# A filler stream with one gate/up tile fewer: its work moves to the seven-product stage, its order and its rate change

## The chip, the cores and the metric

The kernel runs on one core of one Trainium2 chip. The metric is the time of one execution in device microseconds (us). Three runs of the kernel before gave a median of 1049.95 us, between 1048.82 and 1053.6 us. A core has five engines that run side by side and wait for each other through semaphores: PE (TensorE, the matrix unit), DVE (VectorE), ACT (ScalarE), POOL (GpSimd) and SP (SyncE, which here only issues DMAs). In the profile, PEld is the loading of weights into PE.

## The reference: what is computed

One transformer block whose two branches are added: sliding-window attention and a gated feed-forward part, both on the same normalized input.

```python
def _A_ref(x, wqkv, wo):                       # S = 2048 tokens, D = 640, H = 32 heads of Dh = 20
    q, k, v = split(x @ wqkv)
    scores = einsum("bhqd,bhkd->bhqk", q, k) * Dh ** -0.5
    mask = (i - j >= 0) & (i - j < 256)        # causal window of 256
    p = softmax(where(mask, scores, -1e9))
    return reshape(einsum("bhqk,bhkd->bhqd", p, v)) @ wo
def _B_ref(x, w_gate, w_up, w_down):           # Df = 1728
    return (gelu(x @ w_gate) * (x @ w_up)) @ w_down
xn = layernorm(x)
return x + _A_ref(xn, ...) + _B_ref(xn, ...)
```

## The kernel before

**Numbers.** Weights and activations are split into a high and a low part, and each dense product is three matmul passes: high times high, low times high, high times low. A dense product of one 128-column weight tile with one chunk of C = 512 tokens has a depth of 640 = 5 x 128, so it is 15 matmuls of 512 columns (`dense_steps`, L102, its matmul in L106). There are NC = 4 chunks.

**Tiles of weights.** The q and k projections are 10 tiles, worked off in pairs ("qk", i): q tile i and k tile i + 5. The gate and up weights are NF = 14 tiles of 128 columns each (the last, 13, holds the 64 left over of both). One full gate/up tile over all four chunks costs 2 x 4 x 15 = 120 dense matmuls in the plain way.

**Stages in order of time.** First the layer norm, the transposes and the first projections (about 0 to 96 us). Then the attention (about 96 to 550 us). Then what is left of the feed-forward products ("gate/up stage", 550 to 809 us). Last, the down and the output projections (`ps` in L1216, from 809 us on).

**The attention stage** (`attention`, L802) is written out by hand for PE, ACT, DVE and POOL. It has NU = 32 units, one for each of 8 groups of four heads and 4 chunks of tokens; a unit has NS = 14 slots. In a unit PE does four kinds of small matmuls: `ps_m` (L491, raw scores from which DVE takes a maximum, L501), `ps_n` (L518, moves the maxima into place; ACT then sends them to the q rows by a DMA, L521), `ps_e` (L556, shifted scores, of which ACT makes P with an exponential, L558) and `ps_o` (L599, P times V, `av_unit`, called in slot 0 of the next unit). Twelve `ps_e` pieces of a unit come two at a time in the odd slots. POOL blanks the masked corners of P (`clear`, L571 and L574) in the slot after, and adds the two halves of the result (`join`, L609).

**The filler.** Between these small matmuls PE is given dense products from a generator, `filler` (L689): each slot pulls RATE / NS of them (`pull_fill`, L797), 31.2 for a unit; a matmul of 320 columns counts 0.65. `filler` yields in this order: two projections that are left over, then `sets`: the q/k pairs 1, 2, 3, the gate/up tile 0, the q/k pair 4, the gate/up tiles 1 and 2. The products for V of the second half of the heads (`ps_v`) come in when slot V1_SLOT = 169 is past. The weights of the next set are split by ACT and POOL in the meantime (`split_later`, L630; L635, L640), alternately into two pools (`pools`, L686). A q/k product is followed by two ACT steps, one of DVE and one of POOL (`save_qk`, L247; POOL's is L258) and a store to DRAM by SP (L267); a gate/up product by steps of ACT and DVE (`gate_up_fill`, L645). On top POOL forms sums of activations for the next stage, three steps in a unit (`x_sums`, L726; L737, stored in L741).

**Queues.** SP issues its DMAs in program order: the results of the previous unit (L613, L614), the stores of q/k products (L267), the sums (L741), and, in slots 9 and 12, the k and the q rows of unit u + 3 (`load_stack`, L457; L466), which the maxima of that unit read first in slot 5 of unit u + 1. POOL works its list in order too.

**The gate/up stage.** The tile that is split last in the filler (13) is done in the plain way (`gate_up`, L864). Tiles NFA = 3 to 12 are done by `gate_up_pair` (L931; matmuls in L949): for two chunks together, seven products of sums of blocks take the place of eight. It has 6 + 9 + 6 + 9 + 6 + 9 + 9 = 54 dense matmuls for a pair of chunks, and 108 for a tile.

```python
    sets = [("qk", 1), ("qk", 2), ("qk", 3), ("gu", 0), ("qk", 4)]
    sets += [("gu", f) for f in range(1, NFA)] + [("gu", NF - 1)]
    ...
                if i == 0 and u:
                    av_unit(u - 1)
```

Of the kernel before, what the change touches and what calls it, by code (L numbers as in the profile page):

```python
# [28 lines left out]
SR = 3 * DH  # L29
QROWS = 64 + SR  # L30
NS = 14
RATE = 31.2
V1_SLOT = 169
MXD = 7
KSLOT = 9
LAG = 3, 5, 4, 4, 4, 4, 3, 3, 4, 3, 2, 1, 1, 1
NFA = 3
HD = D // 2
HR = 5
NQD = 9  # L40
# [26 lines left out]
def block_kernel(ctx, tc, x, wqk, wv, wgu, wdo, wdl, out):  # L67
# [131 lines left out]
    def at(slot, fn, *a):  # L199
        acts.setdefault(slot, []).append((fn, a))  # L200
# [9 lines left out]
    def flush():  # L210
        while lates:
            fn, a = lates.pop(0)
            fn(*a)
# [118 lines left out]
    def run(*gens):  # L332
        for gen in gens:
            for _ in gen:
                pass
# [121 lines left out]
    def load_stack(u, which=(0, 1)):  # L457
        g, c = divmod(u, NC)
        for m in range(80 * g // 128, (80 * g + 79) // 128 + 1):
            assert all((m + 5 * i, c) in done for i in which), (u, m)  # L460

        for i in which:
            dst, src, top, again = ((qs[u % NQ], qd[c], 1, 2), (ks[u % NK], kd[c], 0, 0))[i]
            for j in (0, 2):
                for p, part, n in ((j * 32, top, 2), (j * 32 + 2 * DH, again, 1), (64 - j * 32, 0, 3)):
                    nc.sync.dma_start(dst[p:p + DH * n, j:j + 2].rearrange("p j t -> p (j t)"),  # L466
                                      src[g, part:part + n].rearrange("s (d j) t -> (s d) (j t)",
                                                                      j=4)[:, j * C:(j + 2) * C])
# [150 lines left out]
    def load_gu(f):  # L619
        raws = []  # L620
        for i in range(2 if f < NF - 1 else 1):
            raw = wrp.tile([128, KT, 128], F32, name="wr", tag="wr")
            nc.sync.dma_start(raw, wgu[2 * f + i])
            raws.append(raw)
        return raws
# [55 lines left out]
                                   lambda k: xh[:, k, cs], lambda k: xl[:, k, cs], KT)  # L681
            defer(1, *((late, c4) if i else (c1,)))

    sets = [("qk", 1), ("qk", 2), ("qk", 3), ("gu", 0), ("qk", 4)]
    sets += [("gu", f) for f in range(1, NFA)] + [("gu", NF - 1)]
    pools = (wp, None), (hp, 2)  # L686
    rest = []
# [91 lines left out]
    NU = NG * NC  # L779
# [4 lines left out]
    def pull_max(n, slot):  # L784
        for _ in range(n):
            x = next(stream, None)
            if x is None:
                return
            max_pair(*x)
            if x[1] == 7:  # L790
                at(slot + (MXD if slot >= 0 else 4), max_end, x[0])

    def tick():
        todo = [y for t in sorted(t for t in acts if t <= now[0]) for y in acts.pop(t)]
        return sorted(todo, key=lambda y: y[0] is max_end)

    def pull_fill(n):  # L797
        debt[0] += n
        while debt[0] > 0:
            debt[0] -= next(fill, 1.0)  # L800

    def attention():  # L802
        now[0] = -1
        load_stack(0)
        load_stack(1)
        load_stack(2)
        for i, (p, k, half) in enumerate((p, k, half) for p in range(NC // 2) for k in range(2) for half in range(2)):
            for j, fn in enumerate(x_sums(p, k, half)):
                m = 10 * i + j
                at(NS * (XS0 + m // XSN) + m % XSN, fn)  # L810
        for i in range(12):
            now[0] = i - 13
            for fn, a in tick():
                fn(*a)
            if i % 2 == 0:
                pull_max(2, now[0])
            flush()
            pull_fill(2 * RAMP)
        pull_fill(GAP)
        for u in range(NU + 1):  # L820
            for i in range(NS):
                T = now[0] = NS * u + i
                for fn, a in tick():
                    fn(*a)
                if i in (0, 5, 9) or T == 3:
                    pull_max(2, T)
                if i == 0 and u:
                    av_unit(u - 1)
                    flush()
                    pull_max(2, T)  # L830
                if i % 2 and i < 12 and u < NU:
                    exp_piece(u, i - 1)
                    if i == 1 and u:
                        pull_fill(1)
                        debt[0] -= 1
                    exp_piece(u, i)
                flush()
                if u + 3 < NU and i in (KSLOT, 12):
                    load_stack(u + 3, (int(i == KSLOT),))
                pull_fill(RATE / NS)  # L840
        while acts:
            now[0] += 1
            for fn, a in tick():
                fn(*a)
            flush()
        now[0] = None
        run(fill)
        assert not acts
# [446 lines left out]
    order.__enter__()  # L1295
    raws_w = load_gu(NFA)
    banks = [psg.tile([128, C], F32, name="ps_g", tag=f"g{i}") for i in range(4)]
# [32 lines left out]

    raws_next = {NFA + 1: load_gu(NFA + 1)}
    for j, f in enumerate(range(NFA, NF - 1)):
        end = f + 1 == NF - 1
# [166 lines left out]
```

## Time and profile before

The profiled execution took 1055.0 us, and its span from the first to the last instruction was 1053.2 us.

| what | value |
|---|---|
| median of three runs | 1049.95 us (1048.82 to 1053.6) |
| profiled execution, its span | 1055.0 us, 1053.2 us |
| granted PE clock, mean of the span | 0.997 |
| busy share of the span | PE 98%, PEld 79%, DVE 70%, ACT 50%, POOL 37% |
| 98 to 550.4 us (attention): PE, ACT, DVE, POOL busy | 447.42, 302.37, 297.18, 328.52 of 452.40 us |
| 565 to 809 us (gate/up): PE, DVE busy | 244.00, 169.03 of 244.00 us |

A busy PE is not a PE at its peak: the profile models the end of a matmul, and matmuls overlap. What one matmul costs is the distance from its start to the next start. In rows of the timeline the columns are start, duration, engine, line, operation, output and inputs, shape and count; in brackets stands how long the engine was idle before, and what ended it. In rows of the chain of waits the columns are start, length, engine, output, line and count.

### The profile page before, as it was taken

What the parts mean: (1) busy time and instruction counts of PE and PEld (TensorE: products, weight loads), DVE (VectorE), ACT (ScalarE), POOL (GpSimd) and SP (SyncE); (2) the same over time, 40 slices, a digit from 0 to 9 for tenths busy, and PEclk for the clock granted to TensorE, in tenths of its full rate; (3) what the DMA queues carried; (4) which work ended last, traced back from release to release, by engine and by line L of the source; (5) the groups of instructions that cost most, each with busy time, mean ns of one, the idle gap of its engine ahead of it and who ended that gap; (6) DMA issues with size and microseconds to landing.
All of it is one profiled execution on the core that took longest, in us unless ns stands there. A gap on an engine that the chain in (4) does not pass through costs nothing.

```text
span 1053.2 us, 25694 instructions
## 1 busy us (share of the span) xinstructions
PE 1037.1 (98%) x9393; PEld 837.1 (79%) x9393; DVE 742.0 (70%) x2018; ACT 528.6 (50%) x1120; POOL 385.6 (37%) x622
## 2 busy tenths in 40 slices
PE   8999999999999999999999999999999999999998
PEld 8878666666787666666668888888888999999998
DVE  7845666667655676677736787776556869888887
ACT  4434766676666667666675232223324544343332
POOL 6021687979665767877460111101110000000000
PEclk9999999999999999999999999999999999999999
DMA  5543355555533344544125576762217874443333
GB/s 198 188 125 99 103 160 161 162 181 153 162 89 106 104 145 125 172 138 155 59 66 192 177 248 207 251 252 110 75 62 254 258 236 131 131 133 115 119 126 105
DMA packets 105192, 158.76 MB, mean 151 GB/s; under 512 B 15420, under 2 KB 60092, under 8 KB 105064
## 3 DMA queue, kind: packets, MB, share of 16 engines
q1 hardware_dynamic: 102680, 150.95, 44.3%
q10 hardware_dynamic: 2384, 6.16, 1.8%
q8 instruction: 74, 1.21, 0.5%
q14 instruction: 54, 0.44, 0.1%
HBM read 101.78 MB, written 54.92 MB: 149 GB/s over the span
## 4 chain that ended last, share of the span: by engine, by line
PE 84%; DVE 7%; DMA 3%; ACT 3%; issue 2%; POOL 1%; SPq 0%; ACTq 0%; DVEq 0%; POOLq 0%
PE ps_g L949 22%; PE ps_d L106 20%; PE ps L1216 16%; PE ps_e L556 8%; PE ps_v L106 6%; PE ps_o L599 5%; PE ps_m L491 4%; DVE junk L501 2%; PE ps_g L106 1%; DVE at L1054 1%; DVE ss L1054 1%; DMA stg<-wtd 1%; DVE wb L1054 1%; PE ps_t L184 1%; DMA qs<-qd 1%
## 5 line engine op out<-in xcount | busy, mean ns | idle before, releaser
L501 DVE CUSTOM_DVE_ANT_0 junk<-ps_m,mask 128x320 bf16<-128x320 f32 (+2 forms) x512 | 242.7, 474 | 132.5 <-PE ps_m L491 75.0
L558 ACT ACTIVATE P<-ps_e 128x512 f32<-128x512 f32 (+2 forms) x384 | 198.8, 571 | 62.1 <-PE ps_e L556 60.1
L1216 PE MATMUL ps<-wb,at 128*128 128x320 f32 x999 | 156.6, 309 | 1.5 <-DVE at L1054 1.4
L1216 PEld LDWEIGHTS ps<-wb,at 128*128 128x128 f32 x999 | 148.9, 188 | 2.4 <-DVE at L1054 1.9
L571 POOL TENSOR_SCALAR_AFFINE_SELECT P<-P 128x256 f32<-128x256 f32 (+1 forms) x192 | 95.4, 501 | 68.5 <-ACT P L558 65.6
L556 PE MATMUL ps_e<-qs,ks 124*128 124x128 bf16 (+2 forms) x704 | 119.0, 278 | 0.5
L106 PE MATMUL ps_d<-xh,wql 128*128 128x512 f32 x310 | 99.3, 424 | 0.0
L106 PE MATMUL ps_d<-xh,wqh 128*128 128x512 f32 x310 | 98.3, 422 | 0.0
L106 PE MATMUL ps_d<-xl,wqh 128*128 128x512 f32 x310 | 98.2, 420 | 0.0
L99 POOL TENSOR_TENSOR wql<-wr,wqh 128x640 fp32r<-128x640 f32 x12 | 19.2, 1607 | 196.1 <-PE ps_g L949 151.0
L1216 PE MATMUL ps<-wt,at 128*128 128x320 f32 x552 | 89.2, 310 | 0.8 <-DVE xr L1239 0.8
L556 PEld LDWEIGHTS <-ks 124*128 124x128 bf16 x704 | 49.6, 98 | 50.3 <-issue 35.3
L574 POOL TENSOR_SCALAR_AFFINE_SELECT P<-P 128x512 f32<-128x512 f32 (+1 forms) x144 | 78.6, 554 | 17.6 <-ACT P L558 15.8
L1216 PEld LDWEIGHTS ps<-wt,at 128*128 128x128 f32 x552 | 82.9, 188 | 1.3 <-DVE xr L1239 1.0
L1170 ACT ACTIVATE at<-ss 128x512 fp32r<-128x512 f32 x59 | 37.3, 632 | 88.1 <-DVE ss L1054 88.1
L599 PE MATMUL ps_o<-P,v 64*32 64x320 f32 (+4 forms) x2816 | 74.8, 347 | 1.7 <-POOL P L574 1.7
L258 POOL TENSOR_TENSOR pt<-r,pt 128x512 bf16<-128x512 f32 x40 | 46.8, 1169 | 70.1 <-ACT pt L254 61.7
L599 PEld LDWEIGHTS ps_o<-P,v 64*32 64x32 f32 x2816 | 50.7, 106 | 23.9 <-POOL P L574 1.6
L491 PE MATMUL ps_m<-ks,qs 60*64 60x320 bf16 (+3 forms) x1472 | 63.2, 260 | 3.8 <-DVE xl L193 1.1
L106 PEld LDWEIGHTS ps_d<-xh,wql 128*128 128x128 f32 x310 | 56.7, 191 | 10.2 <-issue 1.1
L106 PEld LDWEIGHTS ps_d<-xl,wqh 128*128 128x128 f32 x310 | 56.3, 190 | 9.9 <-issue 1.3
L106 PEld LDWEIGHTS ps_d<-xh,wqh 128*128 128x128 f32 x310 | 56.1, 190 | 9.9 <-issue 1.6
(195 smaller groups left out, 1940.8 us busy)
## 6 DMA issues: line engine op xcount, KB each, us to landing
hr<-hd SPq DMA_DIRECT2D x104, 128.0 KB
hd<-he SPq DMA_DIRECT2D x50, 256.0 KB
wr<-wgu SPq DMA_DIRECT2D x27, 320.0 KB
qs<-qd SPq DMA_DIRECT2D x64, 120.0 KB
ks<-kd SPq DMA_DIRECT2D x64, 120.0 KB
xi<-x SPq DMA_DIRECT2D x16, 320.0 KB
qs<-qd SPq DMA_DIRECT2D x64, 80.0 KB
ks<-kd SPq DMA_DIRECT2D x64, 80.0 KB
```

The lines of the kernel that those rows point to most:

```text
L106: nc.tensor.matmul(ps, a(k), b(k), start=n == 0, stop=n == 3 * nk - 1)
L258: nc.gpsimd.tensor_tensor(out=pt[:, l, :], in0=r, in1=pt[:, 1, :], op=OP.subtract)
L491: nc.tensor.matmul(ps[64 * h:64 * h + 64, col:col + w], q[rows, j, q0:q0 + 64], ks_, start=True, stop=True, tile_position=(64 * r, 64 * h))
L501: nc.vector.tensor_tensor_reduce(out=junk[:, 0:n], in0=ps[:, 320 - n:320], in1=mask[:, 320 - n:320], scale=1.0, scalar=NEG, op0=OP.add, op ...
L556: nc.tensor.matmul(ps[:, col:col + n], k[0:QROWS, j, kc:kc + 128], q[0:QROWS, j, q0:q0 + n], start=True, stop=True)
L558: nc.scalar.activation(pt[:, j, lo:hi], ps[:, lo:hi], AF.Exp, scale=SCALE)
L571: nc.gpsimd.affine_select(out=a, in_=a, pattern=[[0, n], [1, 128]], compare_op=OP.is_ge, fill=0.0, base=0, channel_multiplier=-1)
L574: nc.gpsimd.affine_select(out=a, in_=a, pattern=[[0, n], [-1, 128]], compare_op=OP.is_ge, fill=0.0, base=-1, channel_multiplier=1)
L599: nc.tensor.matmul(os[r][32 * j:32 * j + 32, qa:qb], v[rows, w0_:w0_ + 32], pt[rows, j, col + qa - q0:col + qb - q0], start=r not in begun ...
L949: nc.tensor.matmul(ps, i, j, start=first and n == 0, stop=n == len(work) - 1, skip_group_check=True)
L1170: nc.scalar.activation(hi[:, 3:7], s, AF.Copy)
L1216: nc.tensor.matmul(ps[bank][:, 0:HD], *work[bank][j], start=bank not in begun, stop=final[p, bank] == n and j == len(work[bank]) - 1, skip ...
```

## The change

Four edits. NFA is 2 in place of 3: gate/up tile 2 is no longer yielded by the filler, and the loop over `gate_up_pair` starts with it. RATE is 27.2 in place of 31.2. In `sets`, the q/k pair 4 comes ahead of the gate/up tile 0, so that all q/k pairs come first; there is one set fewer, so the pools of weights alternate the other way round from there on. In slot 0 after the last unit, `pull_fill(LAST)` with LAST = 8 is called ahead of the last `av_unit`.

```diff
-RATE = 31.2
+RATE = 27.2
+LAST = 8
 V1_SLOT = 169
 ...
-NFA = 3
+NFA = 2
 ...
-    sets = [("qk", 1), ("qk", 2), ("qk", 3), ("gu", 0), ("qk", 4)]
+    sets = [("qk", 1), ("qk", 2), ("qk", 3), ("qk", 4), ("gu", 0)]
     sets += [("gu", f) for f in range(1, NFA)] + [("gu", NF - 1)]
 ...
                 if i in (0, 5, 9) or T == 3:
                     pull_max(2, T)
                 if i == 0 and u:
+                    if u == NU:
+                        pull_fill(LAST)
                     av_unit(u - 1)
                     flush()
                     pull_max(2, T)
```

## The prediction

> **What bounds the kernel now.** I read the page first, then the busy time by stage, then the waits of PE, then the chain of waits through one attention unit. The first two rows are of the page, the next two of the busy time by stage (a stretch, its length, then busy time and count of each engine, the granted clock, the DMA share), the last three of the waits of PE between 98 and 550 us (total us, times, longest).
>
> ```profile
> span 1053.2 us, 25694 instructions
> PE 1037.1 (98%) x9393; PEld 837.1 (79%) x9393; DVE 742.0 (70%) x2018; ACT 528.6 (50%) x1120; POOL 385.6 (37%) x622
> 98.00:550.40 452.40, 447.42 (x6012) 305.79 (x6010) 297.18 (x1099) 302.37 (x663) 328.52 (x557) 1.00 0.44 132
> 565.00:809.00 244.00, 244.00 (x1077) 201.83 (x1076) 169.03 (x281) 76.04 (x143) 26.89 (x18) 1.00 0.50 175
> PE ps_o L599 <- POOL P L574: 1.7, 2, 1.1
> PE ps_m L491 <- DMA qs<-qd: 0.9, 2, 0.4
> PE ps_m L491 <- DVE mx L501: 0.7, 2, 0.4
> ```
>
> PE is busy nearly throughout in both stages that the change touches, at full clock, and waits for others for only 3.3 us in the attention. Since ends of matmuls are modelled, I check this in the chain of waits, over one unit from `ps_o` to `ps_o`:
>
> ```profile
> 421.49 2.38 PE ps_o L599 x93
> ...
> 431.88 0.54 PE ps_e L556 x4
> 432.42 1.15 PE ps_d L106 x5
> 433.57 0.45 PE ps_e L556 x4
> 434.02 1.39 PE ps_d L106 x6
> ...
> 435.81 0.39 PE ps_o L599
> ```
>
> Every piece is PE's own and each follows where the last ends: the unit (14.32 us) is a sum of PE work. One dense matmul costs 0.23 us in runs of five and six (1.15 / 5 and 1.39 / 6 = 0.232). So four fewer dense matmuls shorten a unit as long as no other engine's answer comes too late. In the gate/up stage one costs 244.00 / 1077 = 0.2266 us, without any gap.
>
> **The change part by part.**
>
> *Tile 2 out of the filler, the lower rate.* 120 dense matmuls leave the attention. The order of the built programs confirms it: 27 or 28 dense matmuls in a unit where 31 or 32 stood, while the other matmuls stand as they did. Gain if PE stays the bound: 120 x 0.232 = 27.8 us, 0.93 us for a unit of four.
>
> *Tile 2 into the gate/up stage.* 108 matmuls at 0.2266 us: 24.5 us more. DVE gets the additions of one more tile: it is busy for 169.03 of 244.00 us there, and does not set the pace. POOL's splitting of one tile moves along, into a stage where it works for 26.89 us. I cost these at nothing: PE's 24 us for a tile cover them, at 169.03 / 10 = 17 us of DVE for a tile; without that cover they would cost DVE's 17 us. The two loads of raw weights only move along SP's queue.
>
> A page gives another price. The Trainium skill (TensorE: Matmul & The Clock Gate, Back-to-back issue gap) states about 216 ns for an isolated warm matmul of 512 columns, wherever it stands; by that the swap would save 12 x 0.216 = 2.6 us and not 27.8 - 24.5 = 3.3 us, an estimate from the page. The trace has 0.2266 and 0.232 us, and decides.
>
> *Dense work ahead of the last P times V.* The timeline of PE, POOL and ACT at the end of the attention, and a row of SP's waits for the next edit:
>
> ```profile
> 544.89 0.70 PE L556 MATMUL ps_e<-qs,ks 124*128 124x128 bf16 x4
> 546.24 2.02 PE L599 MATMUL ps_o<-P,v 64*32 64x320 f32 x52 [0.65 <-POOL P L574]
> 549.34 1.12 PE L599 MATMUL ps_o<-P,v 64*32 64x320 f32 x44 [1.08 <-POOL P L574]
> 550.39 0.96 PE L106 MATMUL ps_g<-xh,wqh 128*128 128x512 f32 x3
> 542.78 1.57 POOL L99 TENSOR_TENSOR wql<-wr,wqh 128x640 fp32r<-128x640 f32 x1 [0.32 <-ACT wqh L98]
> 547.03 1.17 POOL L881 TENSOR_TENSOR wql<-wr,wqh 128x384 fp32r<-128x384 f32 x1
> 549.24 0.59 POOL L571 TENSOR_SCALAR_AFFINE_SELECT P<-P 128x256 f32<-128x256 f32 x1
> 540.01 0.60 ACT L653 ACTIVATE gs<-ps_d 128x512 f32<-128x512 f32 x1
> SPq L466 <- DMA kd<-pt: 5.8, 4, 2.4
> ```
>
> The last `ps_e` begins at 544.89 and `ps_o` at 546.24: 1.35 us, where a block of four takes 0.45, so 0.9 us are lost. `ps_o` then takes until 550.39, 4.15 us, where an undisturbed one takes 2.38: 1.8 us, because POOL splits a weight (L881) ahead of the last blanking. Together 2.7 us. In the changed order seven dense matmuls are left for this place (1.6 us, and not eight), and L881's work comes behind the last blanking. Both causes go, but two ACT steps of the filler's last product (0.6 us each) now stand between exponentials of that unit, which have no spare dense work around them: I give back 0.5 us and take 2.2 us; bounds 0 and 2.7.
>
> *q/k pair 4 first.* By itself no work: it keeps the q and k rows of the seventh head group ahead of their loads at the lower rate. What it removes is small: SP waited 5.8 us in four places for stores of k rows, off PE's path. I cost it at nothing; if the rows were late, PE would wait in `ps_m`, as below.
>
> *What is late next: the loads of q rows.* The attention's slack against SP and POOL shrinks. The busy time in one loaded unit, POOL and SP's queue in it, and PE where it reads the rows; then a place where PE did wait for such a load:
>
> ```profile
> 179.75:193.97 14.22, 14.22 (x204) 9.48 (x207) 9.63 (x37) 10.47 (x21) 13.78 (x24) 1.00 0.59 166
> 186.51 1.29 POOL L609 TENSOR_TENSOR ob<-ob,P 128x512 f32<-128x512 f32 x1
> 189.53 1.16 POOL L258 TENSOR_TENSOR pt<-r,pt 128x512 bf16<-128x512 f32 x1
> 187.83 1.42 SPq L613 DMA_DIRECT2D od<-ob  x4
> 190.72 1.26 SPq L267 DMA_DIRECT2D qd<-pt  x2
> 192.08 2.70 SPq L466 DMA_DIRECT2D ks<-kd  x6
> 194.88 2.16 SPq L466 DMA_DIRECT2D qs<-qd  x6
> 200.40 0.47 PE L491 MATMUL ps_m<-ks,qs 60*64 60x256 bf16 x16
> 164.39 3.09 SPq L466 DMA_DIRECT2D qs<-qd  x6
> 171.65 0.47 PE L491 MATMUL ps_m<-ks,qs 60*64 60x256 bf16 x15 [0.43 <-DMA qs<-qd]
> ```
>
> POOL is busy for 13.78 of 14.22 us. Its late addition (L609) holds SP's stores, its late L258 holds the next ones, and behind them in SP's queue stand the loads of k and q: the q load is issued at 194.88 to 197.04, for a use at 200.40. In the last rows the data came 171.65 - 167.48 = 4.2 us after the last issue, and PE waited. At 200.40 it did not, so the slack there lies between nothing and some 1.4 us. With the change, PE comes to this place earlier by the four matmuls of a unit and about one of the next, 1.2 us. POOL's list gets shorter only by the part that hangs on the filler: at 31.2 matmuls a unit, 2.08 q/k products of 1.16 us and the splitting of weights (240 matmuls take five pieces of 0.47 us four times: 1.2 us a unit), 3.6 us, of which 4 in 31 go: 0.47 us. So up to 1.2 - 0.47 = 0.77 us is lost in such a unit, at least nothing. The group of splitting pieces (470 ns each), and how many units are like this:
>
> ```profile
> POOL 6021687979665767877460111101110000000000
> L640 POOL TENSOR_TENSOR wql<-wr,wqh 128x128 fp32r<-128x128 f32 x65 | 29.5, 470 | 3.3 <-ACT wqh L635 3.3
> 478.31:492.64 14.33, 14.33 (x210) 9.57 (x214) 10.02 (x38) 9.50 (x19) 11.15 (x22) 1.00 0.48 146
> ```
>
> In slices six to ten (26.3 us each, 132 to 263 us) POOL stands at 7 to 9: nine units. The four units of pair 4 come earlier now; I add three, twelve in all (a later unit without q/k products has POOL at 11.15 of 14.33, with room). Bounds 0 and 12 x 0.77 = 9.2 us; I take a third, 3.0 us, since some slack is there and not every unit has two products or a weight to split.
>
> *The exponentials.* `ps_e` has two PSUM banks, so a pair waits until ACT has read the pair before:
>
> ```profile
> 432.30 1.09 ACT L558 ACTIVATE P<-ps_e 128x512 f32<-128x512 f32 x2 [0.27 <-POOL pt L258]
> 433.84 1.09 ACT L558 ACTIVATE P<-ps_e 128x512 f32<-128x512 f32 x2 [0.46 <-PE ps_e L556]
> ```
>
> ACT needs 1.09 us for a pair, starts some 0.3 us after PE (433.84 against 433.57), and with four dense matmuls between the pairs PE returns after 0.45 + 4 x 0.232 = 1.38 us: just in time. The changed order has four dense matmuls at most of these places and three in four units at the last pair, where 0.2 us each is lost: 0.8 us. Bounds 0 and 31 x 0.1 = 3 us, if the places that are just in time give way too. DVE's maxima I cost at nothing: 9.63 us of 14.22 leave room; if not, it is within that 3 us.
>
> *Sum.* -27.8 + 24.5 - 2.2 + 3.0 + 0.8 = -1.7 us. Against the profiled execution (1055.0 us, span 1053.2 us, 1.8 us around it) that is 1053.3 us; it lies 5 us above the median of the runs (1049.95 us), and from the median it gives 1048.2 us.
>
> **The rivals.**
>
> *Clean: no new waits.* -27.8 + 24.5 - 2.2 = -5.5 us, 1044.4 us. For it speaks that PE waits for only 3.3 us today, and that the attention's other engines are at 65 to 73% (297.18 to 328.52 of 452.40 us). Against it, POOL's 13.78 us in loaded units is more than the 13.3 us that a unit would last. The waits that exist, if they vanish too, would bring 1 us more.
>
> *Slower: SP's queue behind POOL sets the unit.* Place: the wait of `ps_m` for the q rows in slot 5. Price: the whole 0.93 us of a unit comes back. If it holds in some 20 of the units with sums and q/k products, 18.6 us come back: -5.5 + 18.6 = +13 us, 1063 us. It decides from twelve units on (11.2 - 5.5 = +5.7 us). For it: the lost microsecond at 171 us already has this form. Against: after it the units run without such a wait, though POOL is as full.
>
> *The attention isn't bound by PE.* Then the removal brings nothing and the added tile costs all: 24.5 - 2.2 = +22 us, 1072 us. For it: PEld is at 305.79 of 452.40 us, 68%, below POOL's 73%. Against: the chain above has only PE in it. The Trainium skill (Perfetto Trace Analysis, Identifying the Most-Contended Engine) bears on this: matmul busy time is no good measure of PE, weight-load busy time is the better one. By that rule POOL would be the engine to relieve; the starts in the chain, without a gap, speak against it here.
>
> *The last edit does nothing.* If the stall at the end only moves, 2.2 us of gain go: 1050.4 us, inside the forecast's span.
>
> **How the numbers follow.** Forecast (part of the gain eaten, between -5 and +5 us) 0.52; clean 0.24; SP behind POOL 0.19; not PE-bound 0.05. A change under 0.5% (5.2 us) is about what a measurement of this kernel can't tell from none. Clean lies just past that bound; I count most of it, 0.22, as faster, the rest and the forecast, 0.54, as the same, the other two as slower, 0.24. The range goes from 1043.4 us (clean, with today's waits gone) to 1058 us, which takes in the upper bounds of loads and exponentials (-5.5 + 9.2 + 3 = +6.7 us) and the beginning of the second rival; past it lie about 0.15.
>
> **What would show it.** Right: units of 13.4 to 13.7 us from `ps_o` to `ps_o`, with the longer ones between 130 and 260 us and a wait of `ps_m` for the q load there; 108 more `ps_g` matmuls at 0.227 us; a last `ps_o` of about 2.4 us. Wrong: units of 14 us with PE waiting for `qs<-qd` or for POOL all along (second rival), units of 13.3 us throughout (clean), or PE idle ahead of the last `ps_o` as before.

## The result, and the profile after

The changed kernel takes 1059.48 us (median of six runs, 1056.78 to 1061.18); the kernel before took 1049.96 us beside it (six runs). The ratio is 1.0078, 95% interval 1.0060 to 1.0096: slower by 0.8%, and outside the range that I gave (1043.4 to 1058.0 us). Later batches, on other occasions, put the kernel before at 1052.95, 1051.92 and 1051.63 us (19, 19 and 27 runs); against those medians the same 1059.48 us would be a loss of 6.5 to 7.9 us, but the changed kernel was not run again beside them. Its six runs fall into two groups, 1056.8 to 1057.9 and 1061.0 to 1061.2 us, and the median lies between them.

The head of the page after, and the busy time by stage (a stretch, its length, busy time and count of PE, PEld, DVE, ACT and POOL, the granted clock, DMA share and rate):

```profile
span 1058.9 us, 25671 instructions
PE 1038.9 (98%) x9381; PEld 836.4 (79%) x9381; DVE 750.7 (71%) x2029; ACT 527.4 (50%) x1120; POOL 380.0 (36%) x614
```

```profile
98.00:531.60 433.60, 424.30 (x5878) 284.58 (x5876) 289.96 (x1079) 293.86 (x647) 319.18 (x547) 1.00 0.44 131
565.00:809.00 244.00, 244.00 (x1079) 202.09 (x1078) 164.57 (x284) 71.44 (x142) 26.44 (x18) 1.00 0.47 162
```

The gate/up stage looks as before: PE without any gap, 244.00 / 1079 = 0.2261 us for a matmul, DVE at 164.57 of 244 us. The attention does not: PE is idle for 433.60 - 424.30 = 9.3 us of it, where it had been idle for 452.40 - 447.42 = 5.0 us. The waits of PE between 96 and 560 us, after:

```profile
PE ps_m L492 <- DVE mx L502: 2.5, 9, 0.4
PE ps_n L519 <- DVE mx L502: 2.3, 3, 1.7
PE ps_m L492 <- DMA qs<-qd: 1.6, 3, 0.6
PE ps_e L557 <- ACT P L559: 0.3, 2, 0.2
PE ps_m L492 <- DVE nm L511: 0.3, 1, 0.3
```

DVE is now the engine that PE waits for most: 2.5 + 2.3 + 0.3 us, where it was 0.7 us. The q rows stand at 1.6 us where they stood at 0.9. The end of the attention in the timeline after (start, duration, engine, line, operation, tensors, shape, count; in brackets idle time and what ended it):

```profile
526.86 0.87 PE L557 MATMUL ps_e<-qs,ks 124*128 124x128 bf16 x4 [0.15 <-ACT P L559]
528.02 1.29 PE L107 MATMUL ps_d<-xl,wqh 128*128 128x512 f32 x5
529.03 0.40 POOL L575 TENSOR_SCALAR_AFFINE_SELECT P<-P 128x256 f32<-128x256 f32 x1
529.24 2.45 PE L600 MATMUL ps_o<-P,v 64*32 64x320 f32 x96
529.96 1.00 POOL L884 TENSOR_TENSOR wql<-wr,wqh 128x384 fp32r<-128x384 f32 x1 [0.17 <-ACT wqh L883]
531.62 0.74 PE L107 MATMUL ps_g<-xh,wqh 128*128 128x512 f32 x2
```

All 96 matmuls of the last `ps_o` follow each other, from 529.24 to 531.62: 2.38 us, where it had been 4.15 us; dense work stands ahead of it, and the splitting of a weight (L884) comes behind the last blanking.

Spans of single executions differ by some microseconds for reasons outside the change: stretches at half clock in the first 70 us, and weights that arrive a little late at about 50 and 65 us of the last stage. So I compare stages, by the starts of PE's matmuls in the timeline, in one profiled execution of each kernel; e1_nolast, which is almost the same program as the changed kernel, repeats its stages up to the down product to 0.3 us. All times in us:

| kernel | first to last `ps_o` | last `ps_o` to gate/up | gate/up | down and output |
|---|---|---|---|---|
| before | 439.0 | 4.2 | 258.7 | 244.1 |
| after | 423.8 | 2.4 | 283.1 | 244.2 |
| e1_nolast | 424.1 | 2.7 | 282.9 | 242.3 |
| e2_lean_after | 421.3 | 2.4 | 283.1 | 244.4 |
| e3_lean_before | 438.0 | 4.1 | 258.7 | 242.4 |
| e4_two_rates | 418.7 | 3.0 | 283.0 | 244.7 |
| e5_nfa_alone | 430.2 | 3.6 | 283.0 | 244.3 |
| e8_hold | 420.6 | 2.4 | 283.1 | 241.7 |
| e9_shift | 431.2 | 2.4 | 283.0 | 243.4 |
| e10_all_but_nfa | 438.9 | 2.4 | 258.6 | 242.4 |
| e11_lean_hold | 420.3 | 2.4 | 283.1 | 243.6 |
| e12_nfa4 | 467.3 | 3.1 | 234.2 | 243.2 |
| e13_two_hold | 419.0 | 3.1 | 283.1 | 242.5 |

The added tile costs +24.4 us (forecast 24.5). Between the first and the last `ps_o` PE has 116 dense matmuls fewer (688 `ps_d` and 804, 240 `ps_v` in both); four more were saved ahead of it. At 0.232 us that is 26.9 us, and 15.2 us came. So 11.7 us of new waits stand in the attention, and the question is which.

To find them I took each piece of PE's work in the 31 units, each from one `ps_o` to the next (a block of `ps_m`, of `ps_e`, of dense work), from its start to the start of the next, and set it against the shortest usual time of pieces of the same kind and size in all the kernels (the lower eighth); what is over is put to the piece that was late. Pieces that are late by less than 0.04 us are left out, so the sum comes to 10.6 us of the 11.7. Sums in us:

| late piece | before | after | e2 lean | e4 two rates | e8 hold | e11 lean, hold | e12 four tiles |
|---|---|---|---|---|---|---|---|
| first maxima of a unit (`ps_m` around `ps_o`; DVE) | 4.7 | 6.9 | 7.0 | 5.0 | 4.6 | 4.6 | 8.1 |
| the maxima's move (`ps_n`; DVE's negation) | 0.1 | 3.0 | 0.5 | 0.4 | 1.2 | 0.5 | 0.0 |
| later maxima (`ps_m`; q rows, DVE) | 1.9 | 4.6 | 4.1 | 3.3 | 5.3 | 6.0 | 1.1 |
| shifted scores (`ps_e`; exponentials) | 6.8 | 9.6 | 10.1 | 12.0 | 9.7 | 9.5 | 5.9 |
| all | 13.6 | 24.2 | 21.7 | 20.6 | 21.0 | 20.8 | 15.5 |

Of the 10.6 us, 8.6 fall in the first twelve of the units (5.7 there before, 14.3 after), which hold most of the q/k products. From `ps_o` to `ps_o`, these twelve last 14.18 us on average in place of 14.34, the other nineteen 13.35 in place of 14.04. Three places of the changed kernel show what the lines mean.

*DVE's list, at the start of the fifth unit.* Rows of the timeline:

```profile
159.80 0.59 ACT L559 ACTIVATE P<-ps_e 128x512 f32<-128x512 f32 x1
160.27 0.60 ACT L277 ACTIVATE pt<-ps_d 128x512 bf16<-128x512 f32 x1
160.98 0.69 DVE L273 TENSOR_TENSOR r<-ps_d,pt 128x512 f32<-128x512 f32 x1 [1.09 <-ACT pt L277]
163.42 0.29 PE L492 MATMUL ps_m<-ks,qs 60*64 60x320 bf16 x1 [0.26 <-DVE mx L502]
164.06 0.33 PE L492 MATMUL ps_m<-ks,qs 60*64 60x320 bf16 x3 [0.35 <-DVE mx L502]
```

A step of DVE on a filler product (L273) stands in its list ahead of the maxima. It needs ACT's L277, which stands in ACT's list behind the exponentials. DVE stands still for 1.09 us; then this step takes 0.69 us while scores whose product began at 160.57 stand ready behind it, and PE pays when it comes back for the second block of `ps_m`. DVE has time enough; its list does not let it use that time.

*A negation, in the eleventh unit.*

```profile
250.81 0.87 POOL L641 TENSOR_TENSOR wql<-wr,wqh 128x128 fp32r<-128x128 f32 x2
251.42 3.70 DVE L511 TENSOR_SCALAR nm<-mx 128x16 bf16<-128x16 f32 x1
251.63 1.28 POOL L610 TENSOR_TENSOR ob<-ob,P 128x512 f32<-128x512 f32 x1
252.87 0.46 POOL L641 TENSOR_TENSOR wql<-wr,wqh 128x128 fp32r<-128x128 f32 x1
253.28 0.64 POOL L572 TENSOR_SCALAR_AFFINE_SELECT P<-P 128x512 f32<-128x512 f32 x1
253.87 1.22 POOL L575 TENSOR_SCALAR_AFFINE_SELECT P<-P 128x512 f32<-128x512 f32 x2
255.79 0.22 PE L519 MATMUL ps_n<-identb,nm 128*128 128x128 bf16 x1 [1.65 <-DVE mx L502]
```

The DVE instruction of 128 x 16 numbers lasts 3.70 us, and ends (255.12) when POOL's unbroken row of work ends (255.09). Its usual time is in the view of the tile `nm` (count, then shortest, middle and longest in ns), first before, then after:

```profile
L510 DVE TENSOR_SCALAR nm<-mx x32: 174/175/1203, 80.7 to 526.1; 128x16 bf16<-128x16 f32 x32
```

```profile
L511 DVE TENSOR_SCALAR nm<-mx x32: 174/176/3704, 79.2 to 508.4; 128x16 bf16<-128x16 f32 x32
```

What releases it can be counted. The traces of the fourteen kernels hold 864 such small steps of DVE (`nm<-mx` and, right behind it, `nm<-mx,nm`). 242 of them last 0.256 us or more: a POOL instruction was running at the start of every one of these, and every one ends 0.025 to 0.037 us after the end of a POOL instruction, in 236 cases of one that ran at its start. The other 622 last 0.174 to 0.185 us: at their start POOL was idle, or had at most 0.15 us left of its instruction. So a negation that starts under a POOL instruction lasts until that instruction ends. Six, this one among them, were held over one or more further POOL instructions that followed without a pause; why these and not others stays open.

*The q rows, in the fourth unit.* The chain of waits (start, length, what):

```profile
150.62 3.50 DMA qs<-qd
154.11 0.14 issue
154.25 0.47 PE ps_m L492 x11
```

The chain goes through a load of q rows, issued at 150.56 us and needed 3 us later. The timeline shows why SP came to it so late:

```profile
141.08 0.63 ACT L255 ACTIVATE pt<-r 128x512 bf16<-128x512 f32 x1
141.85 1.29 POOL L641 TENSOR_TENSOR wql<-wr,wqh 128x128 fp32r<-128x128 f32 x3
143.09 1.16 POOL L259 TENSOR_TENSOR pt<-r,pt 128x512 bf16<-128x512 f32 x1
144.28 1.76 SPq L268 DMA_DIRECT2D kd<-pt  x3
```

ACT's part of a k product is done at 141.71, but three splits of a weight stand ahead of it in POOL's list; SP waits 2.6 us for POOL's part, then stores the product, and issues the loads of k and q behind it almost without a pause until 152.27. This is the wait that the prediction had named, by the path that it had named.

### The profile page after: what moved, and what is told of

Read it like the earlier page. It is cut to its first block, busy times and chain, and to the rows that moved or that the text cites. A ratio compares the mean times of both kernels' runs of the same rounds, so it can differ in the third digit from the quotient of the medians.

```text
span 1058.9 us, 25671 instructions
## 1 busy us (share of the span) xinstructions
PE 1038.9 (98%) x9381; PEld 836.4 (79%) x9381; DVE 750.7 (71%) x2029; ACT 527.4 (50%) x1120; POOL 380.0 (36%) x614
## 4 chain that ended last, share of the span: by engine, by line
PE 83%; DVE 8%; ACT 4%; DMA 3%; issue 2%; POOL 0%; ACTq 0%; DVEq 0%; SPq 0%
PE ps_g L952 25%; PE ps L1219 17%; PE ps_d L107 15%; PE ps_e L557 7%; PE ps_v L107 6%; PE ps_o L600 5%; PE ps_m L492 4%; DVE junk L502 2%; ACT P L559 2%; PE ps_g L107 1%; DMA qs<-qd 1%; DVE ss L1057 1%; DMA hr<-hd 1%; ACT pt L277 1%; DMA out<-xr 1%
## 5 line engine op out<-in xcount | busy, mean ns | idle before, releaser
L572 POOL TENSOR_SCALAR_AFFINE_SELECT P<-P 128x256 f32<-128x256 f32 (+1 forms) x192 | 92.5, 486 | 61.1 <-ACT P L559 59.6
L100 POOL TENSOR_TENSOR wql<-wr,wqh 128x640 fp32r<-128x640 f32 x13 | 20.8, 1601 | 217.3 <-PE ps_g L952 172.4
L107 PE MATMUL ps_d<-xh,wql 128*128 128x512 f32 x270 | 87.8, 425 | 0.0
L107 PE MATMUL ps_d<-xh,wqh 128*128 128x512 f32 x270 | 87.5, 424 | 0.0
L107 PE MATMUL ps_d<-xl,wqh 128*128 128x512 f32 x270 | 85.9, 420 | 0.0
L492 PE MATMUL ps_m<-ks,qs 60*64 60x320 bf16 (+3 forms) x1472 | 66.5, 260 | 6.5 <-DVE mx L502 2.5
L981 ACT ACTIVATE hr<-hr 128x512 f32<-128x512 f32 x22 | 13.9, 632 | 111.2 <-DVE hr L955 111.2
L600 PEld LDWEIGHTS ps_o<-P,v 64*32 64x32 f32 x2816 | 50.8, 106 | 21.7 <-issue 0.9
L492 PEld LDWEIGHTS <-qs 60*64 60x64 bf16 x1472 | 29.8, 105 | 48.0 <-issue 39.6
L952 PE MATMUL ps_g<-xh,wql 128*128 128x512 f32 x198 | 66.3, 389 | 0.0
```

The source lines that it names most:

```text
L107: nc.tensor.matmul(ps, a(k), b(k), start=n == 0, stop=n == 3 * nk - 1)
L492: nc.tensor.matmul(ps[64 * h:64 * h + 64, col:col + w], q[rows, j, q0:q0 + 64], ks_, start=True, stop=True, tile_position=(64 * r, 64 * h))
L572: nc.gpsimd.affine_select(out=a, in_=a, pattern=[[0, n], [1, 128]], compare_op=OP.is_ge, fill=0.0, base=0, channel_multiplier=-1)
L600: nc.tensor.matmul(os[r][32 * j:32 * j + 32, qa:qb], v[rows, w0_:w0_ + 32], pt[rows, j, col + qa - q0:col + qb - q0], start=r not in begun ...
L952: nc.tensor.matmul(ps, i, j, start=first and n == 0, stop=n == len(work) - 1, skip_group_check=True)
```

## The experiments

**Less work for POOL, and so for SP behind it.** Six of the ten POOL steps of `x_sums` are left out, so that the sums lack the low parts, in the changed kernel and in the kernel before.

```diff
 def s2():
-    pool(live[1], live[1], el[:, k, b], OP.add)
+    pass
 # likewise in s3, s5, s7, s9, s10: the terms of the low parts
```

> The changed kernel with six of the ten POOL steps of each sum of activations left out (the sums, and so the output, are incomplete; their stores to DRAM stay). POOL has about 1.3 us less to do in a unit that forms sums. Theory 1 (in the first eleven units POOL's list, and SP's queue behind it, is too long for a unit of 13.4 us): most of the loss there goes, the units 1 to 11 come down from 14.1 to about 13.5 us on average, and the kernel takes 1051 to 1054 us. Theory 2 (the dense products end at other slots than those the delays were set for, and so DVE's and ACT's in-order lists meet the maxima and exponentials at a worse place, whatever POOL does): 1057 to 1060 us, units 1 to 11 at about 14.

> The kernel before with the same six of ten POOL steps left out (its output is incomplete too): the control. Theory 1: little to win, since the units of 14.3 us hold POOL's list: 1046 to 1050 us, so that the two lean kernels stand 2 to 6 us apart, where the full ones stand 9.5 us apart. Theory 2: the same 1046 to 1050 us, but still 9 us less than the lean changed kernel.

Measured: 1057.8 us, ratio 1.0061 (1.0043 to 1.0080), in the changed kernel; 1052.45 us, ratio 0.9998 (0.9980 to 1.0015), in the kernel before. The attention got 2.5 us shorter in the one and 1.0 us in the other. The table says where: the held negation is gone (3.0 to 0.5 us), everything else stays. At the same place of the program:

```profile
251.30 1.30 POOL L610 TENSOR_TENSOR ob<-ob,P 128x512 f32<-128x512 f32 x1
252.46 0.58 DVE L511 TENSOR_SCALAR nm<-mx 128x16 bf16<-128x16 f32 x1
252.55 0.46 POOL L641 TENSOR_TENSOR wql<-wr,wqh 128x128 fp32r<-128x128 f32 x1
253.60 0.64 POOL L572 TENSOR_SCALAR_AFFINE_SELECT P<-P 128x512 f32<-128x512 f32 x1 [0.58 <-ACT P L559]
```

POOL has a pause from 253.01 to 253.60, and the negation ends at 253.04. In both kernels its end lies 0.03 us behind POOL's. The wait for q rows stays, at 1.2 us in place of 1.6. The three splits of a weight (1.29 us) stand ahead of POOL's step in this run too, since the edit leaves them in; so it doesn't clear POOL's list of that wait. Taking out POOL's steps gives back 2.5 of the 11.7 us, or 1.5 us more than in the kernel before. That is what the second theory expected; the kernel before came out above what both expected, with no difference that can be told.

**The rate of the kernel before in the first twelve units.** The same filler at 31.2 in the first twelve units and 24.8 in the others.

```diff
-RATE = 27.2
+RATE = 31.2, 24.8
 ...
-                pull_fill(RATE / NS)
+                pull_fill(RATE[u >= 12] / NS)
```

> The changed kernel with two rates of the filler: 31.2 dense matmuls a unit in units 0 to 11, as before, and 24.8 after, so that as many are pulled in all. Theory 1: the early units go back to 14.3 us with the stalls of the kernel before (about 5 us of stalls in place of 14), the late units have light POOL work and fall to about 12.9 us: 1050 to 1053 us. Theory 2 (products end at the wrong slots wherever the rate isn't 31.2): the early part gains about 8 us, the late part loses as much: 1057 to 1061 us.

Measured: 1055.65 us, ratio 1.0032 (1.0018 to 1.0047). This lies between the two ranges. It takes back 3.8 us of the loss in the median, and in the attention 5.1 us (4.4 us with the last `ps_o`, which takes 3.0 us here). In the table the first maxima and the negation are nearly as before (5.0 and 0.4 us, where 4.7 and 0.1 stood), and the q rows are in time but once:

```profile
PE ps_m L492 <- DMA qs<-qd: 0.4, 1, 0.4
```

The exponentials pay, 12.0 us in place of 9.6, since only three dense matmuls stand between the pairs in many late units. So the early units' waits hang on the pace of the filler in those units: with the products of q and k as early as before, counted in units, they go. The run doesn't tell these earlier products from the longer units, which give every list more time.

**The same products, two slots earlier.** Four more dense matmuls are pulled ahead of the first unit, two slots' worth at 27.2 / 14 = 1.9 a slot, and the rate is lowered so that the filler ends at the same place. The work in a unit is the same.

```diff
-RATE = 27.2
+RATE = 27.075
-GAP = 16
+GAP = 20
```

> The changed kernel with four dense matmuls more pulled ahead of the attention (GAP 20 in place of 16) and the rate lowered from 27.2 to 27.075, so that the last unit gets as many as in the changed kernel. Every product of the filler ends two slots sooner, and load and work are the same. Theory 2: the waits in the first eleven units move to other units and places (those of units 4 and 5 after P times V go), and their sum (13.8 us in the changed kernel) comes out between 9 and 17 us: 1055 to 1063 us. Theory 1: the same units lose as much as before, within a few tenths, 1058 to 1061 us.

Measured: 1066.84 us, ratio 1.0134 (1.0109 to 1.0160), 7.4 us above the changed kernel, as in the attention (7.4 us), and above both ranges. Part of it is not the waits themselves. Rows of the busy time by stretch; the granted clock is the third number from the end:

```profile
140.00:152.00 12.00, 12.00 (x188) 7.95 (x187) 8.74 (x33) 7.96 (x17) 11.80 (x21) 1.00 0.38 106
152.00:155.70 3.70, 1.53 (x7) 0.76 (x6) 1.45 (x5) 1.28 (x4) 1.54 (x3) 1.00 0.53 156
155.70:162.50 6.80, 5.98 (x38) 3.62 (x39) 2.27 (x9) 2.05 (x6) 1.79 (x2) 0.50 0.57 170
```

```profile
PE ps_m L492 <- DMA qs<-qd: 5.7, 6, 1.8
```

PE waits for the q rows at about 152 to 155.7 us, is busy for 1.53 of 3.70 us, and then works at half clock for 6.8 us; a second such stretch of 3.4 us follows at 244 us. Half of 10.2 us is 5.1 us at most, so that at least 2.3 us of the 7.4 are waits (the listed waits of PE sum to 10.2 us, where they were 7.0 us) and the rest is the clock behind them. Two negations are held here as well, one for 2.83 us at 272.92 and one for 3.56 us:

```profile
L511 DVE TENSOR_SCALAR nm<-mx x32: 174/176/3560, 77.5 to 515.5; 128x16 bf16<-128x16 f32 x32
```

What follows: where in the slots a filler product ends decides over microseconds at equal work, and a long wait can cost the clock behind it too. Earlier is not better by itself: the products end two slots sooner here, and PE waits longer for the q rows.

**DVE's filler steps behind the maxima.** A DVE step on a filler product that falls into slot 13 is put behind the maxima of slot 0.

```diff
 def late(fn, *a):
     if now[0] is None or now[0] < NS:
         fn(*a)
+    elif now[0] % NS == NS - 1:
+        at(now[0] + 1, late, fn, *a)
     else:
         lates.append((fn, a))
```

> The changed kernel where DVE's steps on the filler's products that fall in slot 13 are put behind the two pairs of maxima of the next slot 0, not ahead of them; nothing else. In the changed kernel's trace DVE stands idle for 1.1 to 1.4 us ahead of such a step, for ACT, in five units (4, 5, 10, 19, 23 counted from the first P times V), and the maxima behind it keep PE waiting for 0.5 to 0.8 us each after P times V. Theory 2 (in-order lists meet the maxima at a worse place): these waits go, 2 to 3 us less, 1055 to 1058 us. Theory 1 (only POOL and SP): no difference, 1058 to 1061 us.

Measured: 1058.4 us, ratio 1.0059 (1.0042 to 1.0075). The attention is 3.2 us shorter. The medians, which are of different batches, show 1.1 us of it, and 1058.4 us stands where the two ranges meet; so the trace decides here, and not the time. The waits of the units that had such a step fall (sixth unit 1.00 to 0.32 us, eleventh 2.18 to 0.48, twentieth 0.76 to 0.58, twenty-fourth 1.05 to 0.47), the fifth keeps 1.09 us at its first maxima, because there the step isn't in slot 13. In the eleventh the long hold is gone too: with DVE earlier, the two negations there take 0.41 and 1.08 us.

**Both.** The lean POOL and the moved steps together.

> The changed kernel with both: the six POOL steps of the low parts left out (the output lacks those parts of the sums) and DVE's steps of slot 13 behind the maxima of slot 0. From the first P times V to the first ps_g: 426.1 us in the changed kernel, 423.7 with the lean POOL, 422.9 with the moved DVE steps. If the held negation of the eleventh unit (about 1.8 us) is what the two have in common and the rest is separate: 426.1 - 2.4 - 3.2 + 1.8 = 422.3 us. If the two gains add up whole: 420.5 us. If the early rows of q and k are what is left (later maxima, 3.7 us in the first twelve units), they stay as they were with either.

Measured: 1056.31 us, ratio 1.0037 (1.0024 to 1.0051); 422.7 us from the first `ps_o` to the gate/up stage. That is the first case: the held negation is what the two gains have in common. The first maxima and the negation stand at 4.6 and 0.5 us, beside 4.7 and 0.1 us before, so that 4.8 of the 5.1 us that they had lost are back, while the later maxima rose from 4.6 to 6.0 us. Left are 12.2 us in the first twelve units in place of 5.7, the later maxima first of all (6.0 us), where PE waits for q rows:

```profile
PE ps_m L494 <- DMA qs<-qd: 2.1, 4, 0.7
```

**The negation on ACT.** To take it away from DVE, ACT forms it.

```diff
-                nc.vector.tensor_scalar(nm[:, 0, 0], mx, -1.0, None, op0=OP.mult)
+                nc.scalar.activation(nm[:, 0, 0], mx, AF.Copy, scale=-1.0)
```

> The changed kernel with the first of the two small negations of the maxima (128 x 16, before on DVE) made by ACT. In the changed kernel's trace this DVE instruction takes 0.18 us mostly, but 3.70 us once and 0.5 to 1.3 us eight more times, while POOL works. Theory 3 (DVE is held by POOL there and the maxima behind it come late): about 2 to 4 us less, 1055 to 1057 us, with no wait of 1.7 us ahead of the product that moves the maxima. If the hold only moves to the second negation, or ACT's list pays for it: 1058 to 1061 us.

Measured: 1104.88 us, ratio 1.0504 (1.0481 to 1.0527). This is far above what was expected, and it tells nothing of the hold: ACT now stands still for DVE's maxima, in each unit, and the exponentials behind it are late. Waits of ACT and of PE between 96 and 600 us:

```profile
ACT nm L511 <- DVE mx L502: 59.4, 31, 2.7
```

```profile
PE ps_e L557 <- ACT P L559: 35.4, 33, 2.3
```

It shows the same thing at a larger price: one instruction that waits, in the wrong list, costs 45 us.

**The other two edits, without the tile.** The kernel before with pair 4 ahead of tile 0, and with LAST = 8 at 30.75 a unit, which leaves the dense work for the end; NFA stays 3.

```diff
-RATE = 31.2
+RATE = 30.75
+LAST = 8
-    sets = [("qk", 1), ("qk", 2), ("qk", 3), ("gu", 0), ("qk", 4)]
+    sets = [("qk", 1), ("qk", 2), ("qk", 3), ("qk", 4), ("gu", 0)]
```

> The change without its main part: NFA stays 3, the q/k pair 4 goes first, and eight dense matmuls are kept for the last P times V, with a rate of 30.75 for that. PE has the same work as in the kernel before. If the end of the attention is worth what the prediction took (2.2 to 2.7 us) and 0.45 matmuls less in a unit cost no new waits: 1047 to 1049.5 us against 1050 to 1051 us, the last P times V at 2.4 us in place of 4.15. If the slots where products end decide (theory 2), new waits may take that back: 1050 to 1053 us.

Measured: 1050.97 us, ratio 0.9998 (0.9979 to 1.0017): no difference that can be told. The last `ps_o` is 2.4 us in place of 4.2, with fourteen dense matmuls ahead of it; the units' waits are 12.7 us. The end's gain of 1.8 us is there, and too small beside the scatter of the runs (1048.82 to 1056.55 us).

**The tile alone.** The kernel before with NFA = 2 only, at 31.2 a unit.

```diff
-NFA = 3
+NFA = 2
```

> Only NFA is changed (2 in place of 3), the rate stays 31.2, so the filler is empty after unit 27 and the last four units have no dense matmuls. All theories: units 0 to 26 as before, 24.4 us more in the gate/up stage, and the last four units show what the other engines need for a unit when PE has nothing to fill with. PE's own small matmuls take about 7 us there; if ACT sets the pace with its 12 exponentials and some 1.5 us of other steps, 9 to 10.5 us a unit. Four such units save about 4 x 4.5 = 18 us of the 27.8: 1053 to 1060 us.

Measured: 1065.49 us, ratio 1.0125 (1.0085 to 1.0165). This is above the range. At that rate the filler runs out four units early. The last three units take 11.86, 9.78 and 10.16 us, with waits for the exponentials in nearly every pair (488 to 536 us):

```profile
PE ps_e L556 <- ACT P L558: 3.6, 14, 0.5
```

A row of the busy time by stretch shows the clock there:

```profile
495.50:505.70 10.20, 7.85 (x95) 4.03 (x99) 7.08 (x26) 3.36 (x9) 3.51 (x9) 0.50 0.31 96
```

Without dense work a unit can be done in about 10 us, though PE works at half clock for 10.2 us of this end, from 495.5 us on, and for 3.4 us more from 533 us on. This doesn't show what holds a loaded unit: the filler's steps on the other engines are gone as well (POOL is busy for 6.58 us and DVE for 7.43 us of the unit of 9.78 us, against 13.13 and 9.70 us in the seventh unit of the changed kernel). A filler that ended early was worse here than one at a lower rate.

**Without the last edit.** LAST = 0 in the changed kernel.

> The changed kernel without its last edit: nothing is pulled ahead of the last P times V. In the order of the program this moves one dense matmul only, from ahead of the last P times V to behind it: six are left there in any case, since at 27.2 a unit the filler doesn't run out before the end as it did at 31.2. If the short end (last ps_o 2.4 us instead of 4.15) comes from the rate and not from that edit: last ps_o at 2.4 us again and the same stage to within 0.3 us. If the edit makes it: ps_o back at about 4 us and the stage 2 us longer. One look, for the trace.

Measured, one run: 1060.34 us. The timeline at the end:

```profile
529.46 1.07 PE L107 MATMUL ps_d<-xl,wqh 128*128 128x512 f32 x4
530.47 2.45 PE L600 MATMUL ps_o<-P,v 64*32 64x320 f32 x96
532.84 0.50 PE L107 MATMUL ps_d<-xl,wqh 128*128 128x512 f32 x1
```

Six dense matmuls still stand ahead of the last `ps_o`, and it takes 2.4 us. The edit itself moves one matmul; the short end comes from the rate, at which the filler doesn't run out. The program is the same otherwise, and its longest negation is 3.71 us, where the changed kernel had 3.70; so the hold is no accident of one execution. The tile `nm`:

```profile
L511 DVE TENSOR_SCALAR nm<-mx x32: 174/175/3710, 80.2 to 509.9; 128x16 bf16<-128x16 f32 x32
```

**The other direction.** Four gate/up tiles in the filler at 34.75 a unit, the rest as in the changed kernel. (A unit gets 3.6 dense matmuls more than before, not one, as the text on record has it; its sum goes by all 120.)

```diff
-RATE = 27.2
+RATE = 34.75
-NFA = 2
+NFA = 4
```

> The other direction: four gate/up tiles in the filler (0, 1, 2, 3 ahead of 13) at 34.75 dense matmuls a unit, so about one more in each unit than before; pair 4 first and the dense work ahead of the last P times V as in the changed kernel. 120 dense matmuls more in the attention at 0.232 us are +27.8, 108 fewer in the gate/up stage -24.5, the end without its stall -2.0. Theory (a product that ends later, counted in units, makes the lists of DVE, ACT, POOL and SP late, so the waits fall when the rate rises): the waits of the first twelve units, 5.7 us before, fall below 3, and the load of the q rows that PE waited for in the fifth unit (1.5 us) is in time; with some 2 us less for exponentials (more dense work between the pairs) the whole comes to -3, about 1047 us beside 1050. Rival (the waits of before are a floor that the filler doesn't touch): +1.3, about 1051 us, with the waits of the units at 13 us as before.

Measured: 1054.22 us, ratio 1.0031 (1.0016 to 1.0046). Theory and rival both miss in part. As the theory had it, no wait for q rows is left, the negation costs nothing and the later maxima fall to 1.1 us. But the first maxima of a unit rise to 8.1 us. This row alone is left of PE's waits from 96 to 580 us:

```profile
PE ps_m L492 <- DVE mx L502: 2.7, 9, 0.4
```

I read this as the lists in another phase once more: the third unit loses 1.46 us and the sixth 1.79 us there, and the latter is followed by 3.4 us at half clock. In all 15.5 us of waits, with the clock's loss in them, so the price of the swap (+27.8 - 24.5) isn't paid back. Both directions are slower than the kernel before.

**The two remedies together.** The two rates and the moved steps.

> The changed kernel at 31.2 dense matmuls in the first twelve units and 24.8 later, and DVE's steps of slot 13 behind the maxima of slot 0. With the two rates alone 421.7 us from the first P times V to the first ps_g, 1055.65 us in all, of which waits at a unit's first maxima were 5.0 us. Theory (those waits are DVE's order): they fall by 1 to 2 us, 420.2 us for the stage and some 1054.3 in all; with the waits that are left this is still above the kernel before, as 27.8 us of dense work saved there pay for 24.5 elsewhere and the waits of the exponentials grow. Rival (the late units wait for ACT alone): no change, 421.7 and 1055.7 us.

Measured: 1055.01 us, ratio 1.0028 (1.0013 to 1.0043); 422.1 us from the first `ps_o` to the gate/up stage (421.7 without the moved steps). Waits at the first maxima fell from 5.0 to 3.9 us, and other places gave it back. That is nearer to the rival. I read what is left at this rate as ACT's; no run shows it. No version that I tried beats the kernel before.

## Why the prediction was wrong

**What was right.** The tile in the gate/up stage: 24.5 us forecast, 24.4 measured, PE without a gap. A dense matmul in the attention still costs 0.232 us where nothing waits: the chain of waits after has, in the middle of the attention,

```profile
433.35 0.93 PE ps_d L107 x4
434.28 0.47 PE ps_e L557 x4
434.75 1.16 PE ps_d L107 x5
```

The end: 2.2 us forecast, and `ps_o` is 1.8 us shorter. The 0.9 us ahead of it did not come: the pieces of the last unit are late by 1.5 us before and by 1.3 us after, now at the exponentials. But I put the gain to the last edit, and e1_nolast shows that the rate makes it.

**The step that failed.** It is the sentence "DVE's maxima I cost at nothing: 9.63 us of 14.22 leave room; if not, it is within that 3 us". Room was there, and it did not help: DVE works its list in order, and a step that waits for ACT, or that is held, makes the maxima late. First maxima (4.7 to 6.9 us) and the negation (0.1 to 3.0 us) cost 5.1 us more than before, though DVE's busy time from the first to the last `ps_o` fell from 287.6 to 283.1 us. That it is the order and the hold, e11_lean_hold shows: it moves DVE's steps and shortens POOL's list, and 4.8 of the 5.1 us go. The units of 13.4 to 13.7 us that were forecast came from the thirteenth on (13.35 us), and not in the first twelve (14.18 us). A share of busy time, 68%, can't tell this; what could have was each DVE step that has to wait for another engine directly ahead of the maxima, and how much later PE comes for them. The page of before even had the form of it: "PE ps_m L491 <- DVE mx L501: 0.7, 2, 0.4", and its negations of up to 1203 ns stand in the view of `nm`, which the prediction did not use.

**Terms that were right in kind and off in size.** The q rows: 3.0 us forecast with bounds 0 and 9.2, measured 2.7 us at most (all later maxima, 1.9 to 4.6 us). The reason given, POOL's list and SP's queue behind it, is seen at 150 us; the lean POOL left the splits of weights standing there, and no run takes them out. The earlier rate brought the rows in time but once, and earlier products at the same rate (e9_shift) made them later; so why they are late in sum is argued and not shown. The reading that led to twelve units was a little off: POOL's row has a 6 for the eighth slice, where the text says 7 to 9. The exponentials: 0.8 us forecast with bounds 0 and 3, measured 2.8 us (6.8 to 9.6): the places that were "just in time" gave way too, as the upper bound had it. No run was made on them alone, but in the table they follow the rate: 5.9 us at 34.75 dense matmuls a unit, 6.8 at 31.2, 9.6 at 27.2, and 12.0 where the late units have 24.8.

**The sum with measured terms.** -27.8 + 24.4 - 1.8 (last `ps_o`) + 10.6 (waits found) + 1.1 (waits below 0.04 us each) = +6.5 us. The profiled spans differ by 1058.9 - 1053.2 = 5.7 us; the execution after had 0.9 us less of half clock at its start. For the stretch from the first to the last `ps_o` my forecast of waits was 3.0 + 0.8 + 0.5 - 0.9 = 3.4 us, and it was 11.7. The upper end of the range added the bounds of loads and exponentials and nothing for DVE. Still, +6.5 us on the median of 1049.95 us would be 1056.4 us, inside it, by luck, since the loads came far under their bound of 9.2 us. The medians differ by 9.5 us, and the 3 us between lie in no stage of the two profiled executions, which are 6.0 us apart (1055.0 and 1061.04 us); the median of three runs around which the range was laid lies 1.7 to 3.0 us under those of the later batches.

**The rivals.** *Clean* is out: 15.2 of 26.9 us came. *SP behind POOL sets the unit* named a wait that is there in three places, not in twenty, and the relief of POOL that was tried did not end it. *Not bound by PE* is out as a whole, since half of the gain came. By weight-load busy time, one of the two measures for PE that the Trainium skill (Perfetto Trace Analysis, Identifying the Most-Contended Engine) names, POOL would be the engine to relieve; that held for 2.5 us of the attention and not for more. The other measure, the arithmetic done as a share of the peak, was not worked out. *The last edit does nothing* was true of the edit and false of the time: the end got shorter without it.

What stays open: why a few negations are held over several POOL instructions where most wait for one; what makes the q rows late in sum; and whether the early units need the earlier products or the longer time. An experiment on the negation by itself, away from POOL's work and not in ACT's list, was not made.

## What to carry to other kernels

Where engines work lists in order, a stage in which PE is busy for 99% can have no reserve: before work is taken out of its cover, go through each list and see which entries wait for another engine directly ahead of entries that PE needs, and how much earlier PE will come for those. A low share of busy time on DVE or ACT is no such reserve. And cover that is moved is best bought where waits are few: here it could not be taken out of the early units, which hold chains from product to store to load, and the 3.3 us of plain PE work that the swap saves were less than what a shift of phase between the lists could cost (7.4 us in e9_shift).

## What was not expected of the hardware

A DVE instruction of 128 x 16 numbers, 0.175 us as a rule, lasted 3.70 and 3.71 us in two executions of nearly the same program, and 3.56 us in e9_shift, while POOL worked without a pause, and 0.58 us where POOL had one. Of the 864 small negations in the traces, the 242 that were long all end 0.025 to 0.037 us after the end of a POOL instruction. The maxima themselves, which read PSUM, kept their 0.49 us beside it.

Behind waits of PE the granted clock fell to 0.50 in the middle of the attention: for 6.8 us at 155.7 and for 3.4 us at 244 us of e9_shift, for 3.4 us at 190.8 us of e12_nfa4 and at 207.9 us of e7_nm_act, and for 10.2 us from 495.5 us on in e5_nfa_alone, where the dense work had run out. Neither the kernel before nor the changed one shows this in its attention. The Trainium skill (TensorE: Matmul & The Clock Gate, Part 1: The HAM clock gate) tells of a window of 3413 ns and of half rate after an idle one. The lengths agree. But PE was not idle in the stretches ahead: it was busy for 1.53 of 3.70 us in e9_shift and for 2.46 of 3.50 us in e12_nfa4.
